# Routed experts in pairs of token blocks, halves without branches, and masks of 128 rows

## The chip, the cores and the metric

The kernel runs on one core of one Trainium2 chip. The metric is the device time of one execution in microseconds (us). Engines are called as in the profile: PE (TensorE matmul), PEld (its weight loads), DVE (VectorE), ACT (ScalarE), POOL (GpSimd), SP (the queue that issues most DMAs).

## The reference

Three steps, one after the other, all in float32: block-causal attention, a dense layer with SoLU and a layer norm for every token, and a top-1 mixture of eight experts.

```python
# attention: 4 batches, 8 heads, 576 tokens, 64 wide; blocks of 64
scores = np.where(block_i >= block_j, scale * q @ k.T, -1e9)
x = softmax(scores) @ v                     # to [2304 tokens, 512]
# dense layer: w_in [512, 1024], w_out [1024, 512]
h = x @ w_in
solu = h * softmax(h)
ln = (solu - mean) / sqrt(var + 1e-6) * g_ln
x = ln @ w_out
# experts: w_gate, w_output_gate [512, 8], w1 [8, 512, 1024], w2 [8, 1024, 512]
e_idx = np.argmax(x @ w_gate, axis=1)
for e in range(8):
    h = np.maximum(x[e_idx == e] @ w1[e], 0)
    out[e_idx == e] = gate_w * eom[:, e] * (h @ w2[e])
```

With the inputs that are timed the eight experts get 0, 320, 64, 512, 768, 64, 270 and 306 of the 2304 tokens.

## The kernel before, in words

Every matrix is held as two half-precision parts, high and low, so that each product is three matmuls (high x high, high x low, low x high). ACT makes the high part (L1325) and DVE the low one (L1328); for one chunk of a second matrix in four POOL does it (L454, L459).

**Attention** works on pairs of heads in groups of scores (`unit`). A group that ends on the diagonal block gets a third matmul (L717) that adds a large negative number to the last 64 columns: the weights are `msel`, one row with ones in its first 64 places, and the moving side is `mneg`, one row of negative numbers.

**Layer 1** (`layer1`) works on 18 tiles of 128 tokens: first product (L902 to L904, 48 matmuls of 512 columns), SoLU with the norm on POOL (L940, L943, L947), transposes (L959), second product (L987 to L989, 24 matmuls of 512 columns), router product (L1027 to L1029). What is written to memory as `x2d` is the two halves of a token's row.

**Routing** (`route`) ranks the tokens of a few tiles by expert and scatters each token's index and gate from POOL to a list `idxd` in memory (L1112), one indirect DMA a tile, tile after tile. When 14 tiles (`EC`) are routed, `order` makes an early table `tab0` on DVE from the counts (L1174 on PE, L1178 to L1229 on DVE); when all 18 are, `items` makes the late table `tab` (L1178 to L1295). A table says for each block of an expert's tokens which matrix it needs and where its list begins.

**The experts** take blocks of 128 tokens. For a block SP loads its list (L1374), POOL gathers the rows (L1380), PE transposes them (L1414), the first matrix is loaded in four chunks of 512 KB and split, and then come the first product (L1437 to L1439, 96 matmuls of 128 columns), the ReLU and split of the hidden layer (ACT L1448, DVE L1451), the second product (L1471 to L1473, 24 matmuls of 512 columns), the scale and the scatter to the output (L1486). Buffers `w1s`, `xg`, `gx`, `hh`, `hl`, `y` alternate between two. The second matrices of all experts are loaded and split once, 32 chunks. 16 whole blocks stand in the program, four of them (`NEARLY`) from the early table, while layer 1 still works on its last tiles. Rests of an expert's tokens up to 64 are "halves" of 64 tokens; they and any further blocks stand behind branches (`when`, `chain`, L1659, L1663). A half's first product has 64 columns a matmul (L1506 to L1508), and its second 16 matmuls of 512 columns (L1537).

The order on each engine is set by a list scheduler, `Plan`: each step has an estimated cost and a priority, and the constants `MJ`, `MW`, `MF`, `MX` say by how much the steps of a block (matrix, rows) come ahead of its products.

## Time and profile before

| what | value |
|---|---|
| median of 3 runs | 774.12 us (768.97, 774.47, 774.12) |
| profiled execution, its own time | 776.15 us |
| its span | 774.40 us |
| mean granted PE clock | 0.931 of full |
| PE busy | 642.06 us |
| DVE busy | 568.51 us |
| ACT busy | 406.74 us |
| POOL busy | 335.00 us |
| DMA of matrices (512 KB each) | 124 issues |

The span is the time that the trace covers; the profiled execution took 1.75 us more than it. Busy times are sums over the span; work of different engines lies beside each other. The granted clock is the share of TensorE's full 2.4 GHz that it was given (the lower level is 1.2 GHz, 0.5).

### The profile page before, as it was taken

The numbers are of one execution on the slowest core, as the hardware profiler recorded it, in microseconds if no ns is written. First come the engines' busy times: TensorE is split into PE (matmuls) and PEld (weight loads), VectorE is DVE, ScalarE is ACT, GpSimd is POOL, SyncE is SP. The second block draws the span as 40 slices with busy tenths as digits, with TensorE's granted clock in tenths as the row PEclk, the third lists the DMA queues.
The fourth block names the chain that finished last, engine by engine and source line by source line (L and its number), as shares of the span: only waits on it lengthen the run. The fifth ranks groups of instructions, "written<-read, shape, count | busy, mean of one in ns | idle before, by whom it ended". The sixth has DMA issues, their size and how long they took to land. (4 is left out here: it accounts for less than half of the span.)

```text
span 774.4 us, 16678 instructions
## 1 busy us (share of the span) xinstructions
PE 642.1 (83%) x5900; PEld 391.7 (51%) x5900; DVE 568.5 (73%) x1251; ACT 406.7 (53%) x912; POOL 335.0 (43%) x343
## 2 busy tenths in 40 slices
PE   2678767889997899999798985788689979998873
PEld 1345443455553455545354543555367756775642
DVE  6789999998788687976854574569866777654663
ACT  4567566546553455554543354465456656643543
POOL 6872574865636534542513124423714332121332
PEclk9999978979999899999899997989979999999887
DMA  9772665789986989865460244587788789774666
GB/s 204 196 193 84 112 182 118 153 145 190 210 162 115 164 161 170 161 122 102 81 117 22 55 134 161 196 290 200 245 298 286 266 297 336 241 245 140 189 207 202
DMA packets 213548, 138.54 MB, mean 179 GB/s; under 512 B 184144, under 2 KB 184272, under 8 KB 213456
## 3 DMA queue, kind: packets, MB, share of 16 engines
q1 hardware_dynamic: 209680, 127.90, 66.5%
q0 software_dynamic: 3776, 9.46, 3.3%
q8 instruction: 52, 0.85, 0.5%
q14 instruction: 40, 0.33, 0.2%
HBM read 92.99 MB, written 10.78 MB: 134 GB/s over the span
## 5 line engine op out<-in xcount | busy, mean ns | idle before, releaser
L1328 DVE SCALAR_TENSOR_TENSOR mem<-mem 128x1024 f16<-128x1024 f32 x112 | 141.1, 1280 | 51.1 <-ACT mem L1325 49.5
L1325 ACT ACTIVATE mem<-mem 128x1024 f16<-128x1024 f32 x120 | 124.9, 1053 | 79.3 <-DMA mem<-in_moe_w_dram 74.0
L459 POOL TENSOR_TENSOR mem<-mem 128x576 f16<-128x576 f32 (+2 forms) x70 | 103.5, 1484 | 17.8 <-ACT mem L579 10.5
L735 ACT ACTIVATE mem<-S,mem 128x192 f32<-128x192 f32 (+4 forms) x160 | 81.5, 515 | 37.9 <-DVE mem L729 31.2
L1437 PE MATMUL S<-mem 128*128 128x128 f16 x512 | 89.3, 222 | 6.1 <-DVE mem L1421 6.1
L1439 PE MATMUL S<-mem 128*128 128x128 f16 x512 | 89.2, 222 | 0.8 <-DVE mem L1328 0.7
L1438 PE MATMUL S<-mem 128*128 128x128 f16 x512 | 89.3, 222 | 0.0
L454 POOL TENSOR_SCALAR mem<-mem 128x576 f16<-128x576 f32 (+2 forms) x65 | 50.4, 779 | 65.1 <-DMA mem<-mem 30.3
L729 DVE TENSOR_REDUCE mem<-S 128x1 f32<-128x512 f32 (+4 forms) x128 | 68.4, 545 | 8.8 <-PE S L715 4.4
L1380 POOL DMA_INDIRECT mem<-x2d,ix x23 | 29.7, 1290 | 81.1 <-PE T L1414 46.0
L987 PE MATMUL S<-mem 128*128 128x512 f16 x144 | 59.4, 413 | 3.0 <-ACT mem L963 1.1
L989 PE MATMUL S<-mem 128*128 128x512 f16 x144 | 58.5, 407 | 2.1 <-DVE mem L966 2.1
L902 PE MATMUL H<-mem 128*128 128x512 f16 x144 | 57.2, 398 | 3.5 <-DVE mem L929 3.5
L988 PE MATMUL S<-mem 128*128 128x512 f16 x144 | 58.9, 409 | 0.0
L904 PE MATMUL H<-mem 128*128 128x512 f16 x144 | 57.2, 397 | 0.0
L903 PE MATMUL H<-mem 128*128 128x512 f16 x144 | 57.1, 397 | 0.0
L1473 PE MATMUL A<-mem 128*128 (+1 forms) x128 | 49.7, 389 | 7.1 <-DVE mem L1451 7.1
L1438 PEld LDWEIGHTS <-mem 128*128 128x128 f16 x512 | 50.9, 99 | 8.0 <-issue 6.7
L1486 POOL DMA_INDIRECT out_dram<-mem,ix x21 | 26.6, 1265 | 64.6 <-ACT mem L1479 52.2
L1437 PEld LDWEIGHTS <-mem 128*128 128x128 f16 x512 | 51.0, 100 | 1.3
L1439 PEld LDWEIGHTS <-mem 128*128 128x128 f16 x512 | 50.9, 99 | 1.3 <-DVE mem L1328 1.3
L1471 PE MATMUL A<-mem 128*128 (+1 forms) x128 | 49.7, 388 | 1.8 <-ACT mem L1448 1.1
(186 smaller groups left out, 1791.9 us busy)
## 6 DMA issues: line engine op xcount, KB each, us to landing
mem<-in_moe_w_dram SPq DMA_DIRECT2D x124, 512.0 KB, 5.3
x2d<-mem SPq DMA_DIRECT2D x22, 256.0 KB, 2.8
mem<-in_q_dram SPq DMA_DIRECT2D x16, 288.0 KB, 4.0
mem<-in_k_dram SPq DMA_DIRECT2D x16, 288.0 KB, 4.5
mem<-in_v_dram SPq DMA_DIRECT2D x16, 288.0 KB, 3.9
mem<-mem SPq DMA_DIRECT2D x32, 144.0 KB, 3.4
mem<-in_moe_w_in_dram SPq DMA_DIRECT2D x8, 512.0 KB, 3.9
mem<-in_moe_w_out_dram SPq DMA_DIRECT2D x8, 512.0 KB, 3.9
```

The source lines that it names most:

```text
L459: nc.gpsimd.tensor_tensor(out=dst, in0=a, in1=b, op=ALU.subtract)
L729: nc.vector.tensor_reduce(out=stt.t[0:M, c : c + w], in_=src, op=ALU.max, axis=AX.X, negate=True)
L735: op("act", c_act(n, 1, 1), lambda: nc.scalar.activation(out=pexp.t[0:M, po : po + n], in_=pt.t[0:M, co : co + n], func=AF.Exp, bias=stt.t ...
L902: nc.tensor.matmul(o, xT[:, 0, c, tk], win[:, 0, c, fs], start=(c == 0), stop=False)
L987: nc.tensor.matmul(x2p.t, lT.t[:, 0, f], wout[:, 0, f], start=(f == 0), stop=False)
L988: nc.tensor.matmul(x2p.t, lT.t[:, 0, f], wout[:, 1, f], start=False, stop=False)
L989: nc.tensor.matmul(x2p.t, lT.t[:, 1, f], wout[:, 0, f], start=False, stop=(f == FC - 1))
L1325: pl.op("act", c_act(1024, sb=1), lambda: nc.scalar.activation(out=hi(), in_=wf.t, func=AF.Copy, scale=sc), r=[wf, *x], w=[key + (0,)], pr ...
L1328: pl.op("dve", c_dve(1024), lambda: nc.vector.scalar_tensor_tensor(out=lo(), in0=wf.t, scalar=sc, in1=hi(), op0=ALU.mult, op1=ALU.subtract ...
L1437: nc.tensor.matmul(o, wh, xh, start=(c == 0), stop=False)
L1438: nc.tensor.matmul(o, wh, xl, start=False, stop=False)
L1439: nc.tensor.matmul(o, wl, xh, start=False, stop=(c == KC - 1))
```

## The change

Five things change together.

- **Pairs.** The 16 whole blocks become eight pairs of blocks (256 tokens). A pair loads and splits its first matrix once, and its first product has 256 columns a matmul; its second product is done for the two blocks one after the other. Two pairs (`NEARLY`) come from the early table, which takes the experts with the most tokens first. `gx`, `hh` and `hl` become single buffers of twice the width, `xg` has four buffers, `y` three, `w1s` still two.
- **Halves.** Five halves (`NHALF`) stand in the program without a branch, with lists that may be empty. Only what goes beyond eight pairs and five halves stands behind branches (two `chain`s at the end), one block at a time.
- **Tables.** They are made on 128 partitions instead of one and have three kinds of entries (pairs, halves, further blocks); the late one has some 65 DVE operations instead of some 40. Lists of experts are shifted (`sh`, `eb2`) so that an expert of an early pair begins on a pair boundary.
- **Masks.** `msel` has 128 rows, of which row 0 holds the ones, and `mneg` 128 rows. The contraction of the mask's matmul is 128 rows instead of one, and the planner's costs of a score group change with it.
- **Planner.** Its constants for the experts are now in its own unit of time instead of in blocks.

```diff
--- before.py
+++ after.py
...
     EC = 14
-    NEARLY = 4
-    NFULL = 16
-    NITEM = NT + E - 1
-    NMAXF = NT + 3
-    NDYN = NITEM - NEARLY
...
+    NEARLY = 2
+    NPAIR2 = 8
+    NHALF = 5
+    NITEM = NPAIR2 + NHALF
+    NLATE = NPAIR2 - NEARLY
+    NBLK = 10
+    NDYN = NLATE + E + NBLK
+    RB = NT + 2
+    EMPTY = E * RB
...
-    MJ = 7.27
-    MW = 1.79
-    MF = 1.66
-    MX = 2.41
+    MJ = 14.54
+    MH = 6.0
+    MW = 13.0
+    MF = 12.1
+    MX = 17.5
+    MT = 3.6
...
-    msel = const.tile([1, P], BF16, name="msel")
-    mneg = const.tile([1, P], BF16, name="mneg")
+    msel = const.tile([P, P], BF16, name="msel")
+    mneg = const.tile([P, BLK], BF16, name="mneg")
...
     for par in range(2):
         tags(a4, f"w1s{par}", 1, [2, KC, F2], F16)
-        for nm in ("xg", "gx"):
-            tags(a4, f"{nm}{par}", 1, [2 * DM], F16)
-        for nm in ("hh", "hl"):
-            tags(a4, f"{nm}{par}", 1, [F2C, P], F16)
-        tags(a4, f"y{par}", 1, [DM])
+    tags(a4, "xg", 4, [2 * DM], F16)
+    tags(a4, "gx", 1, [2 * KC, 2 * P], F16)
+    for nm in ("hh", "hl"):
+        tags(a4, nm, 1, [F2C, 2 * P], F16)
+    tags(a4, "y", 3, [DM])
...
         nc.vector.memset(msel, 0.0)
-        nc.vector.memset(msel[:, 0:BLK], 1.0)
+        nc.vector.memset(msel[0:1, 0:BLK], 1.0)
...
-            cost = 60.0 + sum(2 * c_mm(n) + (27.0 if i else 0) for _, _, ko, n in parts)
+            cost = 20.0 + sum(2 * c_mm(n) + (29.0 if i else 0) for _, _, ko, n in parts)
...
-                      ge(iot["ebase"]), ALU.add), [rk, "iota"], [bb["pf"]])
+                      ge(eb2 if t0 >= EC else iot["ebase"]), ALU.add),
+           [rk, "eb2" if t0 >= EC else "iota"], [bb["pf"]])
...
+        stt(sh, used, float(2 * P), cat, ALU.mult, ALU.subtract, ["sh"], ["used", "cat"])
+        ts(sh, sh, 0.0, None, ALU.max, None, ["sh"], [])
+        tt(sq, pm.rearrange("o p x -> o x p"), row(sh), ALU.mult, ["sq"], ["pm", "sh"], EE)
+        red(rank, sq, ["rank"], ["sq"], EE)
+        op("dve", 75.0, lambda: nc.vector.tensor_tensor(
+            out=eb2, in0=rank, in1=iot["ebase"], op=ALU.add),
+            r=[("tb", "rank")], w=["eb2"], pri=pri)
...
+        def product1(self, f, o):
+            n, gx, w1s = self.n, self.gx, self.w1s
+            fs = slice(f * P, (f + 1) * P)
+            for c in range(KC):
+                xh, xl = (gx.t[:, a_ * KC + c, 0:n] for a_ in range(2))
+                wh, wl = (w1s.t[:, a_, c, fs] for a_ in range(2))
+                nc.tensor.matmul(o, wh, xh, start=(c == 0), stop=False)
+                nc.tensor.matmul(o, wh, xl, start=False, stop=False)
+                nc.tensor.matmul(o, wl, xh, start=False, stop=(c == KC - 1))
...
+            n, hh, hl = self.n, self.hh, self.hl
+            per = min(512 // n, F2C)
+            rd = [(self.gx, t) for t in range(self.nt)]
+            rd += [(self.w1s, c, a_) for c in range(KC) for a_ in range(2)]
+            for g in range(F2C // per):
...
+                for f in range(g * per, (g + 1) * per):
+                    pl.op("pe", 3 * KC * c_mm(n), lambda f=f, hp=hp, g=g: self.product1(
+                        f, hp.t[:, (f - g * per) * n : (f - g * per + 1) * n]),
+                        r=rd, w=[hp], pri=pri)
...
+            n, hh, hl, yp = self.n, self.hh, self.hl, Buf(self.out)
...
+                    wh, wl = (w2v[:, 0:np_, a_, f, :][:, e] for a_ in range(2))
+                    if n == BLK:
+                        nc.tensor.matmul(o, hh.t[:, f, 0:P], wh, start=(f == 0), stop=False)
+                        nc.tensor.matmul(
+                            o, hh.t[:, f, 0:P], wl, start=False, stop=(f == F2C - 1))
+                        continue
+                    nc.tensor.matmul(o, hh.t[:, f, ts_], wh, start=(f == 0), stop=False)
+                    nc.tensor.matmul(o, hh.t[:, f, ts_], wl, start=False, stop=False)
+                    nc.tensor.matmul(o, hl.t[:, f, ts_], wh, start=False, stop=(f == F2C - 1))
...
+    def pri_of(j):
+        return M0 + MJ * min(j, NPAIR2) + MH * max(j - NPAIR2, 0)
+
...
+    for j in range(NITEM):
+        whole = j < NPAIR2
+        sl = Slot(j, 2 * P if whole else BLK, j % 2, j,
+                  "H" if whole or (j - NPAIR2) % 2 else "A")
+        pri = pri_of(j)
+        sl.load_w(pln, pri - MW)
+        sl.split_w(pln, pri - MW)
+        sl.load_x(pln, pri - MX)
+        sl.trans_x(pln, pri - MT)
+        sl.gemm1(pln, pri)
+        sl.gemm2(pln, pri)
...
+    def chain(j, top, n):
...
-    def chain(j, top, whole):
-        when(j, whole, (lambda: chain(j + 1, top, whole)) if j + 1 < top else None)
-
-    chain(NFULL, NMAXF, True)
-    for j in range(NFULL, NMAXF):
-        when(j, False)
-    chain(NMAXF, NITEM, False)
+        with tc.If(there == 1):
+            more(j, n)
+            if j + 1 < top:
+                chain(j + 1, top, n)
+
+    chain(NPAIR2 + E, NPAIR2 + E + NBLK, P)
+    chain(NPAIR2 + NHALF, NPAIR2 + E, BLK)
...
```

Three places show how the order of instructions moves.

The first is on POOL while layer 1 works on its last tiles: L940 to L947 (L941 to L948 after the change) are the norm of a tile, L1112 (L1114) the scatters of indices to `idxd`, L1380 (L1427) the gathers for the early blocks. Before:

```order
L1112 DMA idxd<-pairs,pos 18432x2
L940 TENSOR_SCALAR mem<-mem 128x1
L943 TENSOR_TENSOR mem<-mem,mhalf 128x1
L947 TENSOR_SCALAR mem<-mem 128x1024
L1112 DMA idxd<-pairs,pos 18432x2 x4
L940 TENSOR_SCALAR mem<-mem 128x1
```

and after:

```order
L1114 DMA idxd<-pairs,pos 20608x2 x4
L941 TENSOR_SCALAR mem<-mem 128x1
L944 TENSOR_TENSOR mem<-mem,mhalf 128x1
L948 TENSOR_SCALAR mem<-mem 128x1024
L1114 DMA idxd<-pairs,pos 20608x2
L455 TENSOR_SCALAR mem<-mem 128x1024
L1427 DMA mem<-x2d,ix_79 128x1024 x2
L460 TENSOR_TENSOR mem<-mem 128x1024
L1427 DMA mem<-x2d,ix_80 128x1024 x2
```

One scatter stood ahead of tile 15's norm and four more ahead of tile 16's (the last row of before). Now four stand ahead of tile 15's norm, and between it and tile 16's (the last row) one more scatter, a split on POOL and four gathers.

The second is on PE around `counts` for the late table (L1174 before, L1183 after): L1471 to L1473 (L1543 to L1545) are second products of early blocks, L1083 and L1085 the last ranks. Before:

```order
L1473 LDWEIGHTS mem
L1473 ISA
L1473 MATMUL A_117<-mem 128x512
L1174 LDWEIGHTS ones
L1174 MATMUL T_116<-cum,ones 1x8
L1471 LDWEIGHTS mem
L1471 ISA
L1471 MATMUL A_117<-mem 128x512
```

and after:

```order
L1545 LDWEIGHTS mem
L1545 ISA
L1545 MATMUL H_108<-mem 128x512
L1083 LDWEIGHTS tri
L1083 MATMUL T_106<-ohs,tri 128x16
L1085 LDWEIGHTS ones
L1085 MATMUL T_106<-cum,ones 128x16
L1183 LDWEIGHTS ones
L1183 MATMUL T_105<-cum,ones 128x8
L1543 LDWEIGHTS mem
```

`counts` stands behind more of the early products: before, 144 matmuls of first and 66 of second products of early blocks follow it, after the change 24 of second products, and then the transposes of two late pairs.

The third is on PE at the halves: L1414 (L1464) transposes, L1437 (L1539) products. Before, behind the last whole block that stands in the program, PE loads the table's entry and branches; the L1437 that follows is a further block, which is not taken with these inputs, and the halves stand behind more such branches:

```order
L1414 LDWEIGHTS mem
L1414 MATMUL T_116<-idh,mem 128x128
L1659 TENSOR_LOAD tab
L1663 COMPARE_AND_BRANCH
L1437 LDWEIGHTS mem
L1437 MATMUL S_112<-mem 128x128
```

and after, between the transposes of a half and a second product of the half ahead (L1539, L1540), where only the matrix's place is read from the table:

```order
L1464 LDWEIGHTS mem
L1464 MATMUL T_105<-idh,mem 128x64
L1539 LDWEIGHTS mem
L1342 TENSOR_LOAD tab
L1539 ISA
L1539 MATMUL A_107<-mem 128x512
L1540 LDWEIGHTS mem
L1540 ISA
L1540 MATMUL A_107<-mem 128x512
```

The branch is gone from this place; the two that are left stand behind all halves.

## Rows read from the trace of the kernel before

**Rows 1.** Busy time by stage: us, PE, PEld, DVE, ACT, POOL, PEclk, DMA, GB/s.

```profile
0.00:160.00 160.00, 114.89 (x913) 69.22 (x913) 142.34 (x335) 94.45 (x274) 101.72 (x109) 0.93 0.67 153
160.00:440.90 280.90, 257.23 (x2080) 138.97 (x2080) 209.51 (x582) 139.37 (x424) 126.74 (x142) 0.95 0.73 135
440.90:529.70 88.80, 67.75 (x559) 40.15 (x555) 57.98 (x142) 45.31 (x63) 32.19 (x36) 0.88 0.55 178
529.70:566.00 36.30, 26.36 (x228) 16.46 (x228) 28.46 (x62) 17.77 (x21) 17.60 (x11) 0.90 0.85 258
566.00:711.90 145.90, 136.06 (x1527) 99.78 (x1525) 97.15 (x95) 82.43 (x96) 37.94 (x29) 0.98 0.79 268
711.90:774.40 62.50, 39.78 (x608) 27.10 (x605) 33.07 (x41) 27.41 (x36) 18.80 (x16) 0.83 0.60 190
```

**Rows 2.** Timeline of PE at a mask: start us, us, instruction.

```profile
286.27 0.25 PE L715 MATMUL S<-mem 128*128 128x192 f16 x1
286.45 0.20 PE L717 MATMUL S<-mneg,msel 1*128 1x64 bf16 x1
286.58 0.26 PE L714 MATMUL S<-mem 128*128 128x192 f16 x1
```

**Rows 3.** Timeline of PE between a second and a first product.

```profile
700.09 0.38 PE L1472 MATMUL A<-mem 128*128 x1
...
701.17 0.22 PE L1437 MATMUL S<-mem 128*128 128x128 f16 x1
...
701.45 0.22 PE L1439 MATMUL S<-mem 128*128 128x128 f16 x1
```

**Rows 4.** Stages again, mask instructions (L717) alone: us, PE, PEld, clock, DMA share.

```profile
0.00:160.00 160.00, 10.29 (x49) 4.58 (x49) 0.93 0.67 153
160.00:440.90 280.90, 15.85 (x79) 7.21 (x79) 0.95 0.73 135
```

**Rows 5.** Timeline of PE: counts, last early product, first late one.

```profile
529.74 0.17 PE L1174 MATMUL T<-cum,ones 128*1 128x8 f16 x1
...
558.01 0.38 PE L1473 MATMUL A<-mem 128*128 x1
...
563.25 0.61 PE L1414 MATMUL T<-idh,mem 128*128 128x128 f16 x4 [4.85 <-DMA mem<-x2d,ix]
...
566.02 0.31 PE L1437 MATMUL S<-mem 128*128 128x128 f16 x1
```

**Rows 6.** Timeline of DVE: first and last operation of both tables.

```profile
446.34 0.14 DVE L1178 COPY mem<-T 1x8 f32<-1x8 f32 x1
...
452.13 0.17 DVE L1229 CAST tab<-mem 1x20 int32<-1x20 f32 x1
...
530.93 0.14 DVE L1178 COPY mem<-T 1x8 f32<-1x8 f32 x1
...
549.98 0.18 DVE L1295 CAST tab<-mem 1x84 int32<-1x84 f32 x1
```

**Rows 7.** The page: a group of splits, and the issues of matrices.

```profile
L1328 DVE SCALAR_TENSOR_TENSOR mem<-mem 128x1024 f16<-128x1024 f32 x112 | 141.1, 1280 | 51.1 <-ACT mem L1325 49.5
...
mem<-in_moe_w_dram SPq DMA_DIRECT2D x124, 512.0 KB, 5.3
```

**Rows 8.** Timelines of PE and POOL in the last stage.

```profile
715.14 0.20 PE L1506 MATMUL S<-mem 128*128 128x64 f16 x1 [2.82 <-PEq L1659]
...
765.72 0.96 POOL L1486 DMA_INDIRECT out_dram<-mem,ix  x1 [0.28 <-POOL mem L1558]
```

**Rows 9.** Timeline of POOL: scatters of indices, then a norm.

```profile
447.38 1.10 POOL L1112 DMA_INDIRECT idxd<-pairs,pos  x1 [2.42 <-DVE mem L1156]
...
465.52 0.97 POOL L1112 DMA_INDIRECT idxd<-pairs,pos  x1 [8.03 <-DMA idxd<-pairs,pos]
...
473.67 0.97 POOL L1112 DMA_INDIRECT idxd<-pairs,pos  x1 [7.19 <-DMA idxd<-pairs,pos]
474.71 0.18 POOL L940 TENSOR_SCALAR mem<-mem 128x1 f32<-128x1 f32 x1
```

More of the change, by code (lines that the diff above doesn't have):

```diff
@@ L1125, in t1 @@
         if name not in tb:
[L1126 removed]
+            tb[name] = tba.get("tb", 1, shape)[0]
         return tb[name]
@@ new lines, in items @@
+        for n, (x, key) in enumerate(((g, "g"), (h, "h"), (b, "b"))):
+            lo, hi = kinds[n]
+            running(cg, x, "cg", key)
+            do(lambda x=x, lo=lo, hi=hi: nc.vector.tensor_copy(
+                out=gs[:, lo:hi], in_=row(x, hi - lo)), ["gs"], [key], (hi - lo) * E)
+            tt(past[:, lo:hi], jid[:, lo:hi], row(cg, hi - lo), ALU.is_ge, ["past"], ["cg"],
+               (hi - lo) * E)
+        stt(prom, xat, RB / 2.0, used, ALU.mult, ALU.add, ["prom"], ["xat", "used"])
@@ L1315, in last @@
     def last(j):
-        lost = 127 if j < NEARLY else 64
-        return max(p for p in range(E) if p * (P * EC // E - lost) <= P * j)
+        if j < NEARLY:
+            return j
+        return max(p for p in range(E) if p * (P * EC // E - BLK) <= 2 * P * j)
     def place(j):
-        n = last(j) + 1
+        n = min(last(j), E - 1) + 1
         return (bass.ds(reg(entry(j, 2), ET.PE, n - 1), 1) if j else 0), n
@@ L1386, in load_w, with __init__ @@
-        def load_w(self, pl, pri, tag=lambda c: "w1f"):
-            j = self.j
+        def __init__(self, j, n, par, at, out):
+            self.j, self.n, self.at, self.ix, self.out = j, n, at, ix[at], out
+            self.nt = 2 if n > P else 1
+            self.m = min(n, P)
+            self.w1s = Buf(f"w1s{par}")
+            self.xg = [Buf("xg") for _ in range(self.nt)]
+            self.gx, self.hh, self.hl = Buf("gx"), Buf("hh"), Buf("hl")
+            self.y = [Buf("y") for _ in range(self.nt)]
@@ L1463, in gemm2 @@
-            at = []
-            def mm(part):
-                if not at:
-                    at.append(place(j))
-                e, n = at[0]
-                for f in range(2 * part, 2 * part + 2):
-                    wh, wl = (w2v[:, 0:n, a_, f, :][:, e] for a_ in range(2))
-                    nc.tensor.matmul(yp.t, hh.t[:, f], wh, start=(f == 0), stop=False)
-                    nc.tensor.matmul(yp.t, hh.t[:, f], wl, start=False, stop=False)
-                    nc.tensor.matmul(yp.t, hl.t[:, f], wh, start=False, stop=(f == F2C - 1))
@@ L1475, in gemm2 @@
-            for part in range(4):
-                rd = [(hh, part // 2), (hl, part // 2)] + self.w2_keys(
-                    [part] if j == 0 else range(4))
-                pl.op("pe", 6 * c_mm(512), lambda part=part: mm(part), r=rd, w=[yp], pri=pri)
-            pl.op("act", c_act(512, 1), lambda: nc.scalar.activation(
-                out=y.t, in_=yp.t, func=AF.Copy, scale=ix[j].bitcast(F32)[:, 1:2]),
-                r=[yp, ("ix", j)], w=[y], pri=pri)
-            self.store(pl, P, pri)
@@ L1627, with more @@
         pln.run({"pool": 2000.0, "act": 1500.0, "dve": 1500.0, "sp": 500.0})
-    def more(j, whole):
+    def more(j, n):
         pl = Plan(SLK)
@@ L1655, in more @@
+        sl.gemm2(pl, 4)
         with tc.manual_schedule():
             pl.run()
-    def when(j, whole, then=None):
-        kind = nc.values_load(
-            tab[0:1, 3, j - NEARLY : j - NEARLY + 1], min_val=0, max_val=2,
-            skip_runtime_bounds_check_because="0, 1 or 2 where the table is made",
-        )
-        with tc.If(kind == (1 if whole else 2)):
-            more(j, whole)
-            if then:
-                then()
-    def chain(j, top, whole):
-        when(j, whole, (lambda: chain(j + 1, top, whole)) if j + 1 < top else None)
```

471 lines of the change are left out of this document (211 added, 260 removed).

## The prediction

> **What bounds the kernel now.** I cut the span into stages and read the engines' busy time in each [rows 1]. Up to 160 us VectorE is the fullest engine (142.34 of 160.00). From 160 to 440.9 us it is TensorE (257.23 of 280.90), and again from 566.0 to 711.9 (136.06 of 145.90). Two stages belong to nobody: from the end of tile 13's router product (440.9) to the first product of the first late block (566.0), TensorE is busy 94.10 of 125.10 us (67.75 of 88.80 and 26.36 of 36.30); in the last 62.5 it is busy 39.78. So a change can gain TensorE work in the second and fifth stage, and waits in the other two. The page's chain of waits covers only some per cent of the span, so I argue by stages.
>
> **Part 1: masks of 128 rows.** Before, a score group's third matmul contracts one row (`msel`, `mneg`), the change makes that 128 rows. The timeline at 286 us shows a 192-column product starting at 286.27, the mask at 286.45, the next product at 286.58 [rows 2]. The spacings of starts at 700 us give what ordinary matmuls cost at full clock: from 700.09 to 701.17 lie five steps of 512 columns, 0.216 each, and from 701.17 to 701.45 five of 128, 0.056 each [rows 3]. That is 0.417 ns a column plus 2.5 ns: 64 columns 0.029, 192 columns 0.083. From 286.27 to 286.58 lie one 192-column product and one mask, so the mask costs 0.31 - 0.083 = 0.23 us, 0.20 more than its columns. 49 masks run before 160 us and 79 in the second stage [rows 4]. A full-height mask on the one hand may keep its 0.23 (gain 0), on the other cost 0.029. The products around it have 128 rows and cost the low figure, so I take the low end: 79 x 0.20 = 15.8 us at most. TensorE idles 23.7 us in that stage, waiting for others, and some of the gain becomes more of that: I take **-12** (0 to -20, where the upper figure lets part of the first 49 count). In the first stage VectorE hides the masks: 0.
> The same rows speak on a rule. The mask's weights are loaded in 0.09 (4.58/49), and what costs is around them. The Trainium skill, "TensorE: Matmul & The Clock Gate", section "LDWEIGHTS (loading the stationary operand)", says that a load of 32 rows takes the time of one of 128, since columns count; by that sentence alone the edit is worth 0, which is rival A. Its page "TensorEngine Tiling (Array Packing)", section "Key Properties", says that changing the tiling mode drains TensorE; by that the 0.20 is the drain and goes. No row tells which of them holds.
>
> **Part 2: from tile 13's router product to the first late block.** This is what the pairs cost. Before, `counts` (L1174) stands at 529.74, 88.8 us after 440.9 [rows 5]. TensorE's work between them, counted in its order and priced with the spacings above: layer 1 products 48+96 of 512 columns (31.1 us), 240 first products of 128 columns (13.4), 30 second products (6.5), and transposes, router products and the like (7.6): 58.6, so 30 us are idle or half clock (granted 0.88 [rows 1]). In the change's order 24 more layer 1 products (5.2 us) stand in this stretch, which before ran ahead of tile 13's router product; there are 192 first products of 256 columns at 0.109 (20.9, against 13.4) and 72 second products (15.6, against 6.5): 81.3. With the same 30 us lost, `counts` comes 111.5 after the router product, +22.7.
> What follows is shorter. The table ran on VectorE from 530.93 to 549.98, 19.05 us, between weight splits of 1.21 [rows 6]. In the change's order its 65 operations stand in a row. The 30 of the early table took 446.34 to 452.30, 0.19 each [rows 6]; 65 of those and nine wide ones at +0.15 are 14 to 15 us, against 20.4 from `counts` to the table's end. From there to 566.02 were 15.9 us: index load, gather, transposes that idle 4.85 for the gather [rows 5]. Now both pairs' gathers stand ahead of the first late product, two more of 1.05: 18. So 32.5 follow `counts` instead of 36.3: -3.8. In all +18.9. But tile 13's router product itself comes 5.2 us earlier, for those 24 products now stand behind it: **+13** (+6 if the idle 30 shrink to 23; +25 if they grow).
> What hid the table before were 144 first products and 66 second products of early blocks, done until 558.4 [rows 5]. Now only 24 second products (5.2 us) are left, so TensorE stands idle for some 27 us; that is in the sum already.
>
> **Part 3: the late blocks.** Twelve blocks become six pairs. Their TensorE work per token is the same but for the fixed 2.5 ns of 96 matmuls a pair, 1.4 us in all. A chunk of 512 KB of a first or second matrix costs VectorE 1.28 [rows 7]; 40 chunks fewer are 51 us, and less on ScalarE. In this stage both have slack (97.15 and 82.43 of 145.9), so the splits lie beside TensorE and give nothing by themselves; the 9.8 us TensorE idles there may shrink. `gx`, `hh`, `hl` are now single, so a pair's transposes must wait for the first product ahead of it, with the second product (20.7 us for two) as cover. **-3** (-6 to +5).
>
> **Part 4: halves without branches.** Before, each of five 64-token halves stood behind a branch; the first waits 2.82 us for TensorE's sequencer [rows 8]. They take 711.7 to 763.1, 51.3 us, for 5 x (96 x 0.029 + 16 x 0.216 + 0.4 + lower clock) = 34.3 us of work; the granted clock there was 0.83 [rows 1]. The change's order puts the first products of half 1 ahead of the second product of half 0, no branch between. I take 36: **-15** (-8 if the first matrices come late, a set being 4 x 1.28 = 5.1 us of VectorE behind loads of 5.3 [rows 7], against 7 us a half; -19 if the clock mends too).
>
> **Part 5: the end.** Two branch checks now stand behind the last half, next to its store (issued 765.72 [rows 8]), whose landing ends the kernel as before: **+1** (0 to +3, the 2.82 above being the bound). The Trainium skill, "Runtime: NRT & Kernel Launch", section "Instruction fetch mechanics", says that a taken branch out of the fetched window waits for a fetch of its target; both of these are taken, and by that the end is nearer to +3.
>
> **Sum.** -12 +13 -3 -15 +1 = -16. The profiled execution is 776.15 (span 774.40 [rows 1], 1.75 around it): 760.15. It lies 2.03 above the median of the runs, 774.12, and so the forecast against the median is **758**.
>
> **The rivals.**
> A. The masks keep their price, or the time they free is lost to other engines in the second stage (VectorE 209.51 of 280.90 there). Then -4 and all else as above: 758 + 12 = **770**, within 1%. For it: the 23.7 us of idle time have an owner other than TensorE. Against: the mask's gap of 0.23 is on the busiest engine.
> B. The idle 30 us of part 2 fill with the larger early pairs (+13 becomes 0), since a pair's first products come in longer runs without waits, and the masks give -16: **742**. For it: the granted clock of 0.88 leaves something to win. Against: that stage waits for GpSimd, not for TensorE's own work.
> C. Slower: GpSimd's queue. There each scatter of indices (L1112) waits until the one before has landed: five start from 447.38 to 473.67, 6.6 us apart, the last ones after 8.03 and 7.19 of waiting, and only then tile 16's norm (L940) at 474.71 [rows 9]. In the change's order tile 15's norm stands behind four scatters instead of one, and tile 16's behind five and the four gathers of the two early pairs. If every scatter comes 8.15 us after the one before, as the last did, and each gather waits as long as a scatter for its indices, tile 16's norm comes 10 us later than its slack allows; its layer 1 product and `counts` move by that. The granted clock of 0.88 [rows 1] says that idle stretches cost some products the lower level (1.2 GHz); 20 us of work at it lose 10 more, an estimate. With masks at -4, that is 758 + 20 + 8 = **786**. It decides when the first late product is more than 24 us later than before, after which -16 is gone. Against: tile 15's layer 1 work is wanted late in this stretch, so 18 us behind three more scatters may cost nothing.
> D. The change doesn't do what it says: the experts' counts don't fit eight pairs and five halves, and a further block runs behind a branch. Its load (5.3), splits and 11 us of products add some 23 unhidden: **781**. Against: before ran 16 whole blocks and 5 halves, which 8 pairs and 5 halves hold if the whole blocks come in twos.
>
> **How the numbers follow.** The forecast, 758 with its own range of 750 to 766, has 0.42; A 0.22, B 0.18, C 0.13, D 0.05. A 1% change is 7.7 us, about what this kernel's runs tell from none (768.97 to 774.47): faster is below 766.4, slower above 781.9. Faster is forecast and B, 0.60. A is the same, with a few hundredths of D's lower half: 0.23. C and the rest are 0.17. The range of 738 to 782 holds forecast, A, most of B and D, and leaves out C.
>
> **What would show it.** Masks: starts after a mask as close as after a 64-column product, and 15 us less TensorE time in the second stage. Part 2: `counts` some 22 us later after tile 13's router product, then TensorE idle for about 27 us before pair 2's transposes. Part 3: a pair every 22 us; loads of `in_moe_w_dram` 40 fewer than 124. Part 4: five halves in about 36 us, no idle time ended by TensorE's sequencer. C would show as scatters 8 us apart and a second layer 1 product of tile 15 or 16 that waits for its norm. The prediction is wrong if the early pairs start much later than the early blocks did, which I can't see in the trace of before, or if the late pairs wait for their single buffers.

## The result and the profile after

The change makes the kernel 1.1% slower: ratio 1.0109 to before, 95% interval 1.0071 to 1.0147. The medians of 18 runs each are 781.93 us and 776.10, 0.8% apart. The profiled execution took 781.41 us, its span is 779.70; before, these were 776.15 and 774.40.

The same stages as in [rows 1], cut at the same events (the end of tile 13's router product, `counts`, the first product of the first late pair, the end of the last pair's second product), with the same columns:

```profile
0.00:160.00 160.00, 100.44 (x957) 67.81 (x957) 145.28 (x347) 96.58 (x288) 102.74 (x112) 0.89 0.69 161
160.00:434.10 274.10, 239.23 (x1999) 132.40 (x2000) 208.82 (x564) 134.01 (x405) 125.79 (x144) 0.94 0.66 133
434.10:545.20 111.10, 92.08 (x583) 54.73 (x583) 70.64 (x158) 56.27 (x78) 48.08 (x46) 0.91 0.56 178
545.20:575.10 29.90, 9.22 (x60) 5.54 (x59) 24.73 (x81) 8.55 (x9) 18.13 (x13) 0.64 0.55 176
575.10:715.30 140.20, 132.27 (x940) 88.84 (x938) 61.93 (x69) 53.65 (x68) 26.59 (x24) 0.99 0.52 177
715.30:779.70 64.40, 38.46 (x593) 24.72 (x591) 22.34 (x26) 18.44 (x23) 9.73 (x11) 0.84 0.25 82
```

| stage | before | after | moved | forecast |
|---|---|---|---|---|
| to the end of tile 13's router product | 440.9 | 434.1 | -6.8 | -17.2 |
| from there to `counts` | 88.8 | 111.1 | +22.3 | +22.7 |
| `counts` to the first late product | 36.3 | 29.9 | -6.4 | -3.8 |
| late blocks or pairs | 145.9 | 140.2 | -5.7 | -3 |
| halves, to the last product's end | 51.2 | 48.7 | -2.5 | -15 |
| last product to the end of the span | 11.3 | 15.7 | +4.4 | +1 |

The forecast of the first stage is -12 of the masks and -5.2 of the 24 products that leave it. So three stages came as forecast or better, and three did not: the first by 10.4 us, the halves by 12.5, the end by 3.4. The granted clock shows where TensorE stood idle: 0.64 of full between `counts` and the first late product (0.90 before).

**Masks.** The timeline of TensorE in the changed kernel, to be held against [rows 2]:

```profile
293.79 0.30 PE L716 MATMUL S<-mem 128*128 128x320 f16 x1
293.92 0.19 PE L718 MATMUL S<-mneg,msel 128*128 128x64 bf16 x1
293.95 0.38 PE L715 MATMUL S<-mem 128*128 128x512 f16 x1
```

The 320-column product starts at 293.79, the mask at 293.92, the next product at 293.95. From the first to the last are 0.16 us, of which 320 columns take 0.136 by the spacing of [rows 3]: the mask costs 0.02 to 0.03 instead of 0.23, so all of the 0.20 is gone. Over the 93 masks of each trace that run at the full clock with no wait behind them, the median is 0.028 us, before 0.226. Yet TensorE's idle time up to tile 13's router product grew: in the second stage it is busy 239.23 of 274.10 us, 34.9 idle, where 23.7 were idle before.

**From tile 13's router product to the late pairs.** TensorE's timeline, from the last router product of tile 13 over `counts` and the last early second product to the transposes and the first late product, which answers to [rows 5]:

```profile
433.91 0.17 PE L1030 MATMUL S<-wg,mem 128*128 128x16 f16 x1
...
545.20 0.17 PE L1183 MATMUL T<-cum,ones 128*128 128x8 f16 x1
...
551.12 0.38 PE L1545 MATMUL H<-mem 128*128 x1
...
570.46 1.03 PE L1464 MATMUL T<-idh,mem 128*128 128x128 f16 x8 [18.96 <-DMA mem<-x2d,ix]
...
575.13 0.42 PE L1482 MATMUL S<-mem 128*128 128x256 f16 x1
```

`counts` starts 111.1 us after the end of the router product (434.1), as worked out. The stretch is longer by work and not by waiting: TensorE is busy 92.08 us in it, before 67.75, and stands idle for 19.0, before 21.1. Behind `counts` are 24 second products, then 18.96 us of idle time that end with the gathered rows. On VectorE the late table's first and last operation ([rows 6] are those of before):

```profile
548.64 0.15 DVE L1187 COPY mem<-T 128x8 f32<-128x8 f32 x1
...
561.09 0.20 DVE L1337 CAST tab<-mem 1x96 int32<-1x96 f32 x1
```

The table itself takes 12.6 us instead of 19.2; its start waits 3.4 for weight splits that stand ahead of it. On GpSimd, a scatter of indices and the norms of tiles 16 and 17 ([rows 9]):

```profile
455.33 1.36 POOL L1114 DMA_INDIRECT idxd<-pairs,pos  x1 [6.45 <-DMA idxd<-pairs,pos]
...
484.13 0.40 POOL L941 TENSOR_SCALAR mem<-mem 128x1 f32<-128x1 f32 x1
...
517.89 0.19 POOL L941 TENSOR_SCALAR mem<-mem 128x1 f32<-128x1 f32 x1 [5.29 <-ACT mem L936]
```

Tile 16's norm stands at 484.13, 50 us behind tile 13's router product, where it stood 34 behind it before (474.71). Tile 17's is at 517.89. The scatters' waits did not grow (6.45 here). Tile 16's norm could have started when ScalarE's sum for it was done, at 478.74 (before 464.35): it stood 5.4 us in GpSimd's queue, before 10.4. TensorE's longest wait for such a norm, ahead of the transposes of tile 15 (before, of tile 16), did not grow either: 5.86 us, before 8.10.

**Halves.** ScalarE's timeline at the first half, VectorE's beside it, and TensorE's second product of that half, with the first of its weight loads (PEld):

```profile
717.98 3.90 ACT L1370 ACTIVATE mem<-mem 128x1024 f16<-128x1024 f32 x4 [1.77 <-PE S L1483]
721.78 0.58 ACT L1508 ACTIVATE mem<-S 128x512 f16<-128x512 f32 x1
```

```profile
719.07 4.63 DVE L1373 SCALAR_TENSOR_TENSOR mem<-mem 128x1024 f16<-128x1024 f32 x4
723.62 0.68 DVE L1511 SCALAR_TENSOR_TENSOR mem<-S,mem 128x512 f16<-128x512 f32 x1
```

```profile
724.36 0.10 PEld L1539 LDWEIGHTS <-mem 128*128 128x128 f16 x1 [2.10 <-DVE mem L1511]
...
724.95 0.59 PE L1539 MATMUL A<-mem 128*128 x1 [2.57 <-DVE mem L1469]
725.33 0.63 PE L1540 MATMUL A<-mem 128*128 x1
725.75 0.63 PE L1539 MATMUL A<-mem 128*128 x1
```

The first product of half 0 ends at 718.2. Its ReLU (L1508) stands on ScalarE behind four splits of a first matrix (L1370) that were let go by the same first product, since it frees their buffer; so it starts at 721.78. Its low part (L1511) stands on VectorE behind four more (L1373, 719.07 to 723.70). The weights of TensorE's second product are the hidden layer, and their load waits for that low part; the product's own row names a later operation of VectorE (L1469). So the second product waits until 724.95, and behind the wait TensorE runs at the lower level of its clock (0.50 granted from 724.5 to 727.9): the two products at 725.33 and 725.75 are 0.42 apart instead of 0.22. The same happens at 744.8 (4.01 us). Two more second products wait for their low part, 0.84 and 2.24 us.

**The end.** TensorE's last product and GpSimd's last store ([rows 8]):

```profile
763.64 0.38 PE L1540 MATMUL A<-mem 128*128 x1
...
766.49 0.91 POOL L1580 DMA_INDIRECT out_dram<-mem,ix  x1 [0.28 <-POOL mem L1573]
```

From the store's start to the end of the span are 13.2 us, before 8.7. What stands in the queues there are the two blocks behind branches (L1671) and the program's end (L1703); each row has the count, the shortest, median and longest in ns, and the first and last start:

```profile
L1671 POOLq EVENT_SEMAPHORE  x10: 17/30/2120, 767.3 to 772.4; - x10
...
L1671 PEldq COMPARE_BRANCH  x2: 3322/3666/4010, 761.3 to 765.4; - x2
...
L1671 POOLq COMPARE_BRANCH  x2: 45/45/45, 766.8 to 771.6; - x2
L1671 POOLq INC_SWDGE_SEM  x2: 1372/1380/1388, 769.8 to 772.5; - x2
...
L1703 POOLq DRAIN  x3: 40/107/4979, 773.9 to 779.4; - x3
```

GpSimd's own branches take 0.045 us each. What takes time in its queue is a wait of 2.12 us behind the first of them, an `INC_SWDGE_SEM` of 1.4 behind each, and only then, from 773.9, a `DRAIN` of 4.98 with which the program closes.

**Loads and splits.** The loads fell by 40, as counted; VectorE's splits fell by 36 and 41.2 us in the group that [rows 7] shows:

```profile
L1373 DVE SCALAR_TENSOR_TENSOR mem<-mem 128x1024 f16<-128x1024 f32 x76 | 99.9, 1347 | 22.6 <-ACT mem L1370 22.3
...
mem<-in_moe_w_dram SPq DMA_DIRECT2D x84, 512.0 KB, 4.9
```

### The profile page after: what moved, and what is told of

The parts are those of the page before. It is cut to its first block, busy times and chain, and to the rows that moved or that the text cites. A ratio compares the mean times of both kernels' runs of the same rounds, so it can differ in the third digit from the quotient of the medians.

```text
span 779.7 us, 14588 instructions
## 1 busy us (share of the span) xinstructions
PE 611.7 (78%) x5124; PEld 374.0 (48%) x5124; DVE 533.7 (68%) x1241; ACT 367.5 (47%) x871; POOL 331.0 (42%) x349
## 4 chain that ended last, share of the span: by engine, by line
PE 34%; DVE 29%; issue 12%; POOL 10%; DMA 9%; ACT 4%; SPq 0%; POOLq 0%; ACTq 0%; DVEq 0%
DVE mem L730 4%; DMA mem<-mem 4%; PE H L1543 3%; PE S L1482 3%; PE H L1545 3%; PE H L1544 3%; PE S L1484 3%; PE S L1483 3%; DVE mem L842 3%; PE S L988 2%; PE S L989 2%; PE S L990 2%; POOL mem L460 2%; DVE mem L1373 2%; DVE mem L777 2%
## 5 line engine op out<-in xcount | busy, mean ns | idle before, releaser
L1373 DVE SCALAR_TENSOR_TENSOR mem<-mem 128x1024 f16<-128x1024 f32 x76 | 99.9, 1347 | 22.6 <-ACT mem L1370 22.3
L1370 ACT ACTIVATE mem<-mem 128x1024 f16<-128x1024 f32 x84 | 84.5, 1050 | 34.2 <-DMA mem<-in_moe_w_dram 28.5
L736 ACT ACTIVATE mem<-S,mem 128x512 f32<-128x512 f32 (+4 forms) x160 | 81.6, 515 | 37.1 <-DVE mem L730 26.7
L1482 PE MATMUL S<-mem 128*128 128x256 f16 (+1 forms) x416 | 85.6, 244 | 4.2 <-DVE mem L1469 3.3
L1484 PE MATMUL S<-mem 128*128 128x256 f16 (+1 forms) x416 | 85.5, 244 | 0.8 <-DVE mem L1373 0.8
L1483 PE MATMUL S<-mem 128*128 128x256 f16 (+1 forms) x416 | 85.5, 244 | 0.0
L455 POOL TENSOR_SCALAR mem<-mem 128x576 f16<-128x576 f32 (+2 forms) x65 | 54.6, 845 | 54.8 <-PE A L864 20.0
L1511 DVE SCALAR_TENSOR_TENSOR mem<-S,mem 128x512 f16<-128x512 f32 x37 | 25.3, 689 | 46.4 <-ACT mem L1508 46.4
L830 PE MATMUL T<-idf,mem 128*128 128x128 f32 (+1 forms) x208 | 41.8, 304 | 16.6 <-DVE mem L842 10.1
L1543 PE MATMUL H<-mem 128*128 (+1 forms) x128 | 48.5, 379 | 7.9 <-ACT mem L1577 6.2
L715 PE MATMUL S<-mem 128*64 128x64 f16 (+4 forms) x160 | 47.4, 315 | 2.4 <-ACT mem L736 2.3
L1508 ACT ACTIVATE mem<-S 128x512 f16<-128x512 f32 x37 | 22.0, 597 | 57.8 <-PE S L1484 57.7
L1545 PE MATMUL H<-mem 128*128 (+1 forms) x128 | 48.5, 379 | 0.0
```

The source lines that it names most:

```text
L736: op("act", c_act(n, 1, 1), lambda: nc.scalar.activation(out=pexp.t[0:M, po : po + n], in_=pt.t[0:M, co : co + n], func=AF.Exp, bias=stt.t ...
L1370: pl.op("act", c_act(1024, sb=1), lambda: nc.scalar.activation(out=hi(), in_=wf.t, func=AF.Copy, scale=sc), r=[wf, *x], w=[key + (0,)], pr ...
L1373: pl.op("dve", c_dve(1024), lambda: nc.vector.scalar_tensor_tensor(out=lo(), in0=wf.t, scalar=sc, in1=hi(), op0=ALU.mult, op1=ALU.subtract ...
L1482: nc.tensor.matmul(o, wh, xh, start=(c == 0), stop=False)
L1483: nc.tensor.matmul(o, wh, xl, start=False, stop=False)
L1484: nc.tensor.matmul(o, wl, xh, start=False, stop=(c == KC - 1))
```

## The experiments

Ratios are to the kernel before, timed on the same chip in the same job; brackets hold the 95% interval. Where two ratios are held against each other, their jobs and chips often differ, and with both intervals a difference has some 0.5% of play to either side. A trace is one execution: with the same order on every engine up to there, tile 13's router product ends at 431.1 us in b1 and at 440.9 in n1.

### Masks and planner costs apart

**m1**, the kernel before with 128 rows:

```diff
-    msel = const.tile([1, P], BF16, name="msel")
-    mneg = const.tile([1, P], BF16, name="mneg")
+    msel = const.tile([P, P], BF16, name="msel")
+    mneg = const.tile([P, BLK], BF16, name="mneg")
...
-        nc.vector.memset(msel[:, 0:BLK], 1.0)
+        nc.vector.memset(msel[0:1, 0:BLK], 1.0)
```

> The kernel before with the masks' 128 rows alone, the planner's costs and so every engine's order unchanged. Theory (the masks' time is freed on TensorE, but VectorE and the copies set the pace there): a mask costs 0.03 instead of 0.23 us, TensorE's idle time up to tile 13's router product grows by about what the masks free (15 us), and the time is within 3 us of before. Rival (the masks are worth what they freed, and the new order around them lost it): 760 to 765, and tile 13's router product 12 us earlier than 440.9.

Measured 0.9906 [0.9872, 0.9939], some 7 us faster. Neither theory is right as it stood: of the 15.8 us that the masks free on TensorE in the second stage about half comes out here, and idle time takes 6.4. Its first two stages, cut at tile 13's router product:

```profile
0.00:160.00 160.00, 106.22 (x919) 70.22 (x920) 145.96 (x348) 96.79 (x284) 103.64 (x112) 0.93 0.70 158
160.00:433.20 273.20, 243.11 (x2070) 138.46 (x2070) 204.01 (x569) 136.47 (x414) 126.02 (x140) 0.95 0.73 136
```

The router product comes 7.7 us earlier (433.2), all else shifts with it, and TensorE idles 30.1 us in the second stage, before 23.7.

**m2**, the same with the planner's new costs, **k1**, the kernel before with these costs alone, and **p1**, the change with masks of one row and the old costs:

```diff
-            cost = 60.0 + sum(2 * c_mm(n) + (27.0 if i else 0) for _, _, ko, n in parts)
+            cost = 20.0 + sum(2 * c_mm(n) + (29.0 if i else 0) for _, _, ko, n in parts)
```

> As m1_masks_only, with the change's planner costs for a score group too, so the order is planned anew. Theory (others set the pace): within 3 us of before, as m1. Rival (the re-planned order is what lost the gain): slower than m1 by 8 us or more.

> The kernel before with the planner's new costs of a score group alone (20 and 29 in the place of 60 and 27), masks of one row, blocks as before. Theory (the costs lose by the order that they lead to, whatever the masks are): slower than before by 10 to 20 us, 788 to 798, the late counts 100 us or more behind tile 13's router product instead of 88.8. Rival (the loss needs masks that are cheaper than before, a collision in the first stages): within 4 us of before.

> The change without its masks (one row again, old costs for a score group). Theory (masks are worth next to nothing): 779 to 785, as the change. Rival (the masks hide a larger loss of the pairs): 790 to 797.

m2: 1.0163 [1.0124, 1.0203]. k1: 1.0273 [1.0234, 1.0312]. p1: 1.0055 [1.0026, 1.0084]. So the two numbers in the planner cost 2.6 to 2.7%, some 20 us, with masks of either kind. They change no instruction, only the order in which the engines take them. m2 is 20 us slower than m1, as its rival had it; k1 came above its theory's range, with `counts` 104.7 us behind the router product. p1 falls into the range of its theory by luck: q1, which has the same order and differs in the masks alone, shows that they are worth 1.7%; p1 equals the change because it lacks both their gain and the new costs' loss.

**q1**, the change with the old costs (the lines above, reversed):

> The change with the planner's old costs of a score group (60 and 27), all else of it kept, the masks of 128 rows too. Theory (the new costs, by the order that they lead to, lose what the masks free, as between the two kernels with masks alone, and pairs add a few us of their own): 770 to 776, tile 17's norm on GpSimd back at some 63 us behind tile 13's router product or earlier, instead of 84. Rival (with pairs the masks free nothing): 781 to 785 as the change.

0.9881 [0.9839, 0.9923]: 771.58 us, faster than before by 9 us, and by the ratios 2.3% (18 us) faster than the change, as its theory had it; the two profiled executions are 10.0 us apart (spans of 769.7 and 779.7). Its stages from 160 us to the first late product:

```profile
160.00:431.90 271.90, 239.73 (x2065) 136.66 (x2062) 204.25 (x566) 135.34 (x412) 124.67 (x147) 0.96 0.68 135
431.90:529.80 97.90, 71.52 (x468) 40.88 (x467) 66.37 (x149) 50.68 (x69) 41.51 (x41) 0.90 0.63 196
529.80:565.10 35.30, 21.46 (x144) 13.56 (x143) 28.08 (x87) 13.78 (x16) 17.83 (x14) 0.84 0.67 189
```

From tile 13's router product to `counts` are 97.9 us: 9 more than before and 13 less than with the new costs. The 22.3 that I put down to the pairs are 9 of pairs and 13 of the order. The 13 are work that the new order puts ahead of `counts`, since TensorE is busy 71.52 us there in q1 and 92.08 in the change: 24 more products of layer 1, 60 more first and 24 more second products of early pairs. So the stretch alone overstates the loss; behind `counts` the change gets 5.4 back (29.9 against 35.3).

The ratios side by side:

| | one row, old costs | 128 rows, old costs | one row, new costs | 128 rows, new costs |
|---|---|---|---|---|
| blocks | 1 (before) | 0.9906 (m1) | 1.0273 (k1) | 1.0163 (m2) |
| pairs and halves | 1.0055 (p1) | 0.9881 (q1) | not run | 1.0109 (the change) |

Masks of 128 rows gain 0.9 to 1.7% (7 to 13 us) in each of the three pairs of kernels with the same order; the new costs lose 2.3 to 2.7%; pairs, halves and tables together move the time by 0.6% at most, to either side.

### Is it that low costs mislead the planner?

**c1** to **c4** are the change with other pairs of numbers in that line: 61 and 27, 60 and 29, 30 and 29, 80 and 27.

> The change with the planner's cost of a score group 61 and 27, one unit from the old 60 and 27 of q1_old_costs (ratio 0.988). Theory A (the old pair of numbers stands for one good order among many, and any other number gives one of the others): 779 to 792, like the change, counts over 105 us behind tile 13's router product. Theory B (low costs are what misleads the planner): 769 to 775, as q1_old_costs.

> The change with 60 and 29: the old base with the new price of a masked part. Theory A (any other number): 779 to 792. Theory B (low costs mislead): within 4 us of q1_old_costs, 769 to 775.

> The change with 30 and 29, near its own 20 and 29, but leading to another order at the end of layer 1 (72 second products of layer 1 ahead of the late counts, as in q1_old_costs, instead of 96). Theory A: anywhere in 772 to 792, not tied to the cost being low. Theory B: 778 to 785, as the change.

> The change with 80 and 27, above the old costs. Theory A: 775 to 792, slower than q1_old_costs. Theory B: 765 to 775, as q1_old_costs or faster.

| base and masked part | 60, 27 (q1) | 61, 27 | 60, 29 | 80, 27 | 30, 29 | 20, 29 (the change) |
|---|---|---|---|---|---|---|
| ratio to before | 0.9881 | 1.0228 | 1.0275 | 1.0186 | 1.0401 | 1.0109 |

Every interval is within 0.0053 of its ratio. Theory B is refuted: one unit (a nanosecond of planned time) more than the old base loses 3.5%, 80 loses too, and the time does not go with the number. Theory A has the direction, but c1, c2 and c3 (792.91, 797.84 and 806.45 us) lie above its ranges. The old numbers stood for one good order, and the change's own are the best of the other five. The stretch from tile 13's router product to `counts` in c1, 111.8 us, is as long as in the change:

```profile
443.00:554.80 111.80, 89.63 (x583) 53.79 (x583) 71.47 (x158) 56.24 (x78) 49.68 (x46) 0.91 0.59 177
```

**r4** tries the cause that I saw in the orders, that the early pairs' products stand ahead of layer 1's last tiles and nothing is left behind `counts`:

```diff
+    EW = 4.0
...
-        sl.trans_x(pln, pri - MT)
-        sl.gemm1(pln, pri)
-        sl.gemm2(pln, pri)
+        late = EW if j < NEARLY else 0.0
+        sl.trans_x(pln, pri - MT + late)
+        sl.gemm1(pln, pri + late)
+        sl.gemm2(pln, pri + late)
```

> The change with its new costs, and one priority moved: the transposes and products of the two early pairs rank 4 planner units later, so behind layer 1's last tile. In the order all 96 first and 48 second products of the second early pair then follow the late counts, instead of 24 second products. Theory (the new costs lose by placing early pairs' work ahead of layer 1's last tiles, so that the counts come late and TensorE has nothing to do behind them): counts 95 to 100 us behind tile 13's router product instead of 111, idle time behind the counts under 5 us instead of 19, 768 to 774. Rival (GpSimd's queue makes tile 17 late, whatever TensorE does ahead of it): counts still 108 or more, 779 to 784.

1.0059 [1.0027, 1.0091], not told apart from the change; the theory's time (768 to 774) did not come. TensorE's timeline, `counts` and the first late product:

```profile
537.54 0.19 PE L1184 MATMUL T<-cum,ones 128*128 128x8 f16 x1 [0.47 <-issue]
...
571.96 0.42 PE L1483 MATMUL S<-mem 128*128 128x256 f16 x1
```

`counts` did come 10 us earlier after tile 13's router product (436.5), but the first late product only 5.6, 34.4 behind `counts` instead of 29.9: the gap was closed by moving work into it, and behind `counts` the late rows came no sooner. **q5** does the same to the best order (below):

> The kernel q2_old_costs_halves with the early pairs' transposes and products ranked 4 units later, as in r4_early_later. Theory (as there): the counts 88 to 92 us behind tile 13's router product instead of 96.7, no idle time for the late rows, 750 to 757. Rival (TensorE idles ahead of the counts instead, since what would fill its waits there has been moved away): 758 to 764.

0.9824 [0.9782, 0.9866] against 0.9768 for the kernel it starts from: no gain. `counts` came 91.7 us behind the router product, as the theory said, but 767.22 us is above both ranges. Nor is the rival's mark there: TensorE's idle time ahead of `counts` is 25.0 us, in q2 25.5. What is longer are the six late pairs, 146.6 us instead of 138.3.

### Halves

**h1**, the change with one priority:

```diff
+    MWH = 11.0
...
-        sl.split_w(pln, pri - MW)
+        sl.split_w(pln, pri - (MW if whole else MWH))
```

> The change with one priority moved: the splits of a half's first matrix rank behind the hidden layer of the half two before it (11 instead of 13 ahead of its products). Theory (ReLU and split of a half's hidden layer wait behind four splits of 1.05 and 1.28 us in ScalarE's and VectorE's queues, and TensorE waits for them): the stalls of 2.57 and 4.01 us ahead of second products go, the five halves take 40 to 43 us instead of 48.8, in all 773 to 777. Rival (the first matrices come late from memory): the same 48 to 50 us, 780 to 783.

0.9934 [0.9906, 0.9962], 1.7% faster than the change, as the theory said. The five halves take 40.9 us instead of 48.7; with this priority they take 38.8 to 41.2 in four traces (h1, q2, q4, q5), without it 46.5 to 51.3 in ten. The 7.8 us are 1.0%; where the rest of the 1.7% comes from, the trace does not show. ScalarE's timeline at half 0:

```profile
721.24 0.60 ACT L1509 ACTIVATE mem<-S 128x512 f16<-128x512 f32 x1 [2.06 <-PE S L1485]
721.74 3.88 ACT L1371 ACTIVATE mem<-mem 128x1024 f16<-128x1024 f32 x4
```

The ReLU now starts at 721.24, as soon as the product is done (718.24 to 721.20), and the four splits follow. TensorE's next second product does not wait for it.

**q2**, q1 with h1's priority and two hidden buffers for the halves, cut out of the pairs' one:

```diff
+            if n == BLK and at < NITEM:
+                self.hh = Buf("hha" if out == "A" else "hhb")
...
+        if j == NPAIR2:
+            for i, nm in enumerate(("hha", "hhb")):
+                lo = area["hh"][0][0] + i * 2 * F2C * P
+                pln.tag(nm, [])
+                pln.late(nm, view(lo, [F2C, P], F16)[0], lo, area)
```

> The kernel q1_old_costs with the halves' splits ranked later as in h1_splits_later, and two buffers for the halves' hidden layer in the place of the pairs' one. Theory (both waits of the halves are queues and the one buffer): the five halves take 36 to 38 us, 10 to 14 us less than in q1_old_costs, in all 758 to 765. Rival (the hidden buffer was no wait of its own): 40 to 41 us for the halves, as in h1_splits_later.

0.9768 [0.9734, 0.9803], 761.14 us. The halves take 39.7 us, 9.5 less than in q1 but only 1.2 less than in h1. The time is the theory's, but the halves are the rival's: the single buffer was hardly a wait of its own.

### Idle time behind the late counts, and the end

**n1**, the change with `NEARLY = 3`:

> The change with three pairs from the early table instead of two, five from the late one. Theory (TensorE stands idle for 19 us behind the late counts since it has nothing left): a third early pair fills that, the late products start no later, and the time falls by 12 to 20 us, to 762 to 770. Rival (its 22 us of products run ahead of the counts and push them back by as much): 779 to 785, idle time behind the counts still 15 us or more.

0.9917 [0.9880, 0.9953], 773.03 us, 1.9% faster than the change, though short of the theory's 762 to 770. Behind the last early second product TensorE takes the third pair's transposes, and its first product waits 1.96 us where the change stood idle for 18.96:

```profile
557.52 0.61 PE L1464 MATMUL T<-idh,mem 128*128 128x128 f16 x8
560.08 0.27 PE L1482 MATMUL S<-mem 128*128 128x256 f16 x1 [1.96 <-DVE mem L1469]
```

**q4**, q2 with `NEARLY = 3`:

> The kernel q2_old_costs_halves (old costs, the halves' splits later, two hidden buffers) with three pairs from the early table instead of two. Theory (the wait of 10.4 and 0.95 us for the late pairs' rows behind the early products is still there in q2 and the third pair fills it): 748 to 754. Rival (the counts move back by what the third pair takes): 759 to 763.

0.9718 [0.9674, 0.9761], 756.09 us: the fastest, 2.8% ahead of before, though its gain over q2 is within the intervals and the theory's 748 to 754 was not reached.

**b1**, the change without its last two lines, `chain(...)`. It leaves out the code for further blocks, which these inputs don't need:

> The change without the two chains of further blocks behind the halves; with these inputs no block runs there, so what is left out is only the code and its two branches. Theory (the 4.4 us more between the last product and the end are those two branches over a large body of code): last product to end 10 to 11.5 us instead of 15.7, in all 776 to 778. Rival (the last store's landing sets the end): 15 us as before, 781.

0.9986 [0.9954, 1.0019], 777.85 us, as the theory said. GpSimd's last store, the program's closing `DRAIN`, and the span:

```profile
766.02 0.91 POOL L1580 DMA_INDIRECT out_dram<-mem,ix  x1 [0.28 <-POOL mem L1573]
```

```profile
L1701 POOLq DRAIN  x3: 45/107/6123, 765.8 to 772.4; - x3
```

```profile
core 0: 772.7 us, clock 0.922
```

From the store's start to the end are 6.7 us instead of 13.2: the two blocks behind branches cost 6.5 us, though neither of them runs. Without them GpSimd's `DRAIN` starts at 765.8, ahead of the store, and in the change at 773.9, 7.4 us behind it.

## Why the prediction was wrong, step by step

**The steps that failed.** Two terms make most of the miss. The larger is Part 4's: -15 for the halves, -2.5 measured (below). The other is the price of the new order up to tile 13's router product. There -17.2 was forecast: -12 for the masks and, in Part 2, -5.2 because 24 products of layer 1 stand behind it in the new order. It was taken for granted that work which leaves a stage shortens it by its own time, and that all else stays as before; the line with the two planner numbers got no term. It is this line that moves the 24 products: with the old numbers they stand ahead of the router product. Even so it ends at 431.4 to 433.3 us in the five traces with old numbers and 128 rows (m1, q1, q2, q4, q5), and at 431.1 to 440.9, 435.7 in the mean, in the five with the change's order up to there (the change, h1, n1, r4, b1). So the order gave +3 instead of -5.2 (means of traces that lie up to 10 us apart).

The masks were sized about rightly: 432.3 in the mean of the first five against 440.9 (before) and 445.5 (p1) with one row is -11, and m1 alone has -7.7 for -12. In all, the new numbers cost 18 us by the ratios (q1 against the change; 10.0 between the profiled executions) and 20 in the kernel before (k1). The 13 us of the stretch to `counts` were in the sum all the same, since Part 2 counted its products from the new order; the prediction read that order in three places only and took the rest of it as equal.

**Part 2** gave the right sum for a wrong reason. 111.5 us to `counts` were forecast and 111.1 came, since the count of products was taken from the new order. (The products as listed add up to 80.4, not 81.3, and 18.9 less 5.2 is 13.7, not 13; neither matters to the outcome.) But "this is what the pairs cost" does not hold: 9 us are the pairs', 13 the order's (q1). What follows `counts` was 29.9 us instead of 32.5, because the gathered rows came sooner behind the table (13.8 us from its end to the first late product, 18 forecast), while `counts` to the table's end took 16.1 instead of 14 to 15.

**Part 3** held: 140.2 us for six pairs, 5.7 less than for twelve blocks (-3 forecast), and TensorE is still busy 132.27 of the 140.20. Where the 5.7 us come from no experiment shows; VectorE is busy 61.93 us there instead of 97.15, and it had slack before.

**Part 4**: -15 forecast, -2.5 measured. The branches did go, but the halves took 48.7 us and not 36: TensorE stands idle for 10.1 of them and runs three stretches of 3.4 us at the lower level of its clock. The failed step is that nothing but TensorE's work and the loads was priced: the queues of ScalarE and VectorE were not read. Splits and ReLU are let go by the same first product, the splits rank ahead, and the first and third half wait for them (2.57 and 4.01 us). h1 gets 7.8 of the missing 12.7 us back by one priority; the other 4.9 stay open. The bound of -8, for first matrices that come late, was set for another cause and didn't reach.

**Part 5**: +1 forecast with a bound of +3, +4.4 measured. The two blocks behind branches cost 6.5 us (b1), more than twice the 2.82 of [rows 8] that was the bound: that wait of TensorE's was the wrong row to go by, for the end hangs on GpSimd's queue, where two `INC_SWDGE_SEM`, a wait and a late `DRAIN` stand. The Trainium skill's rule on taken branches ("Runtime: NRT & Kernel Launch", section "Instruction fetch mechanics") pointed to the right side, but for another reason than the trace has: TensorE's second branch takes 4.01 us, which the rule would explain, but is over at 769.5, before GpSimd's second block begins (771.2), while GpSimd's take 0.045 each.

**The rivals.** A came true in part: some of what the masks free became idle time (6.4 us in m1). Its other reading, that a mask keeps its price, is refuted by 0.23 against 0.03, which is what the rule on draining between modes would give ("TensorEngine Tiling (Array Packing)", section "Key Properties", in the Trainium skill); that a drain is what went, no row shows. C gave nearly the right time (786) by the wrong path: the norms of tiles 16 and 17 did come late, but the scatters waited no longer than before, tile 16's norm stood 5.4 us in GpSimd's queue instead of 10.4, and TensorE's wait for such a norm was 5.86 instead of 8.10; the order of TensorE's work, not GpSimd's queue, set it. D has the measured time to within 1 us (781) by luck: no further block ran, for the first products of 64 and 256 columns are those of eight pairs and five halves (L1482 runs 8 x 32 and 5 x 32 times). B's mark is not in the trace.

What stays open is which placement in the poorer orders costs the time. Most of it is lost earlier than I looked. In the change tile 13's router product ends 2.2 us later than in q1 although 24 products, 5.2 us, fewer stand ahead of it: 7.4 of the 10.0 us that the two traces differ by. m2 against m1 (4.8 later, of 20.5 up to the first late product) and k1 against before (5.7, of 23.3) have 10 or 11 by the same count, about half. r4 and q5 moved work that stands behind that point, so they could not settle it; no run changed the order within attention alone.

## What to carry to other kernels

A list scheduler's numbers can stand for one good order. After a change in them, here even of one nanosecond, the order is a new draw, here up to 5% apart; so a change that touches instructions and planner numbers is to be timed in two steps. When branches go, or a buffer is shared, read the queue of every engine that feeds the stage: a step that is let go by the same event as the urgent one must rank behind it. And what a block behind a branch makes the storing engine do behind a kernel's last store is paid in full, even if the block does not run.

## What the runs showed of the hardware

A matmul that contracts one row, between matmuls of 128 rows, costs 0.23 us for 64 columns; with 128 rows it costs 0.03. Of the 15.8 us that this freed on TensorE in its fullest stage, 7 to 13 came out, in three pairs of kernels with the same order. Two blocks behind branches at the end, neither of which runs, cost 6.5 us, with GpSimd's branches at 0.045 each and an `INC_SWDGE_SEM` of 1.4 behind each of them.
